# Attention step of a two-stage MoE kernel: weighted sums moved ahead of the query transpositions, PSUM pairs in rotation

## The chip, the core and the metric

The kernel runs on one core of a Trainium2 chip. The metric is the device time of one execution in microseconds (us). Five engines work beside each other, each in the order of its own instruction list: TensorE (PE in the profile: matrix products and transpositions, its weight loads are PEld), VectorE (DVE), ScalarE (ACT), GpSimd (POOL) and SyncE (SP), which here issues the DMA transfers. They wait for each other through semaphores. PE writes its results to PSUM, eight banks of 2 KB per partition; DVE and ACT read them from there. About 0.2% is what a measurement of this kernel can tell from no change.

## What is computed

The program is an attention with feature maps and, behind it, two mixtures of experts (MoE). The change touches the attention alone, which takes the first 145 us of some 1890. Its reference, for 4 batches, 8 heads, 576 tokens, head size 64 and 128 features:

```python
def phi(x):
    proj = np.einsum('bhsd,df->bhsf', x, w_phi)
    proj = proj - np.max(np.abs(proj), axis=-1, keepdims=True)
    return np.concatenate([np.exp(proj), np.exp(-proj)], axis=-1)
q_p, k_p = (phi(q), phi(k))
kv = np.einsum('bhsf,bhsd->bhfd', k_p, v)
z = np.sum(k_p, axis=2)
num = np.einsum('bhsf,bhfd->bhsd', q_p, kv)
den = np.einsum('bhsf,bhf->bhs', q_p, z)[..., None] + 1e-06
return (num / den).astype(np.float32)
```

Its result, as 2304 rows of 512, goes through a first MoE (all 8 experts on all rows, weighted by a balanced gate) and a second one (each row to its one best expert). These fill the rest of the time.

## The kernel before

The attention is cut into 8 units (two batches and two heads each), and a unit into 3 groups of 384 tokens. One step of the loop at L668 takes one group through every stage of a software pipeline (`step`, L624): the projection of a key group and of a query group (`proj`, L140), and for groups of earlier steps the key-value product (`kvm`, L163), the transposition of the query's projection (`qtr`, L183), the weighted sums (`num`, L195) and the transposition of the finished rows (`xtr`, L211). There are 24 key groups; query groups run two steps behind, so that a unit's key-value product is complete before its queries need it. Steps 4 to 24 of the loop have a `num` in this loop's main part, steps 5 to 24 also an `xtr`; from step 25 on (`live["tail"]`) the stages are interleaved with the first MoE's matmuls and use other PSUM tiles. In the names of tiles k and q stand for key and query; the first number after rk or rq is the unit, the second the group.

What a step makes each engine do:

- PE: k projection (12 records in the profile), q projection (12), key-value products (48 records, or 64 where the middle group of a unit crosses the border of two batches), 6 transpositions of `qtr`, 3 of `xtr`, 48 records of `num`.
- DVE: row maximum and subtraction for the key (`mk`, `prk`, L153 and L154) and the query (`mq`, `prq`), then for `num` the denominator, its reciprocal and the product (`d` and `xn`, L206 to L208). In steps 4 to 9 a few small operations of `misc_comp` come on top.
- ACT: exponentials of the key (`ek`, L158) and the query (`eq`, L192), once per unit two copies of the key-value product (`kvz`, L180), the copy of the transposed rows (`xo`, L218), and from step 12 casts of weights and rows for the MoE (L332, L369).

Before, the order within a step on PE is k, q, `kvm`, `qtr`, `xtr`, `num`. PSUM is used so: two pairs of banks (tag psR, two buffers) take k, q and `qtr` in turn; two single banks (psD) take `xtr` and `num` in turn; one bank each (psC, psB) holds the key-value sums of the unit. A PSUM tile can be given out again only when the readers of its last contents are done; the program puts such waits, and those for inputs, into the instruction that needs them. A tile is what the waits are made for: between two uses of one and the same tile by different engines the program orders the later behind the earlier.

`misc_trans` (L299) transposes an 8-row table of the second MoE once; the loop calls it ahead of step 6.

Of the kernel before, what the change touches and what calls it, by code (L numbers as in the profile page):

```python
# [11 lines left out]
F32 = mybir.dt.float32  # L12
# [9 lines left out]
B, H, S, D = 4, 8, 576, 64  # L22
NT = B * S
DM = H * D
E, FF = 8, 1024
P = 128
NTL = NT // P
KD = DM // P
# [16 lines left out]
def build(tc, a, out):  # L45
# [5 lines left out]
    live = {}  # L51
# [10 lines left out]
    n_ps = [0]  # L62

    def psum(tag, shape):
        n_ps[0] += 1
        bufs = {"A": 4, "B": 1, "C": 1, "D": 2}[tag]
        return live["pp"].tile(shape, F32, tag="ps" + tag, bufs=bufs, name=f"ps{tag}{n_ps[0]}")
# [31 lines left out]
    NG, NC = len(CH), len(CH[0])  # L99
    GW = NC * P  # L100
    S2 = 2 * S
    W = D + 1
# [12 lines left out]
        cs = slice(c0_ * W, c1_ * W)  # L115
        SP.dma_start(out=live["v", u][:, :, cs], in_=a["v"][bp, h_][:, :, cs])

    def heads2(tags):
        if not live.get("tail"):
            n_ps[0] += 1  # L120
            t = live["pp"].tile([P, 2, 512], F32, tag="psR", bufs=2, name=f"psR{n_ps[0]}")[:, :, 0:GW]
            return [t[:, 0], t[:, 1]], [(slice(0, 2), t)]
        ts = [psum(t_, [P, 1, GW]) for t_ in tags]
        return [t[:, 0] for t in ts], [(slice(h_, h_ + 1), t) for h_, t in enumerate(ts)]

    def warm(n):
        ps = psum("D", [P, P])
        for _ in range(n):
            T.matmul(ps, ident, ident, start=True, stop=True)

    wphi = ap_.tile([P, P], F32, bufs=1, name="wphi")
    load_in(0, "k", 0)
    for g in range(2):
# [2 lines left out]
    load_in(0, "k", 1)  # L136
    load_v(0, NC, 10)
    warm(8)

    def proj(u, which, g):  # L140
        r = live.pop(("r" + which, u, g))
        hs, parts = heads2("CB")
        for c in range(NC):
            for h_ in range(2):
                rs = slice(h_ * D, h_ * D + D)
                T.matmul(hs[h_][:, c * P:(c + 1) * P], r[rs, c * P:(c + 1) * P], wphi[rs, :], start=True, stop=True)  # L146
        m = ap_.tile([P, 2, NC], F32, tag="m", bufs=4, name=f"m{which}{u}{g}")
        pr = ap_.tile([P, 2, NC, P], F32, tag="pr" + which, name=f"pr{which}{u}{g}")
        if which == "k" and (u, g) == (0, 0):
            parts = [(slice(h_, h_ + 1), parts[0][1][:, h_:h_ + 1]) for h_ in range(2)]  # L150
        for h_, ps in parts:
            ps = ps.rearrange("p h (c f) -> p h c f", f=P)
            V.tensor_reduce(out=m[:, h_], in_=ps, axis=AX.X, op=ALU.max, apply_absolute_value=True)  # L153
            V.tensor_tensor(out=pr[:, h_], in0=ps, in1=m[:, h_].unsqueeze(3).to_broadcast([P, h_.stop - h_.start, NC, P]), op=ALU.subtract)  # L154
        if which == "k":
            ek = ap_.tile([P, 2, 2, NC, P], F32, tag="ek", name=f"ek{u}{g}")
            for h_, sg in [(h_, sg) for h_, _ in (parts if (u, g) == (0, 0) else [(slice(0, 2), None)]) for sg in range(2)]:
                A.activation(out=ek[:, sg, h_], in_=pr[:, h_], func=AF.Exp, scale=1.0 - 2.0 * sg)  # L158
            live["ek", u, g] = ek
        else:  # L160
            live["pr", u, g] = pr
# [15 lines left out]
    def kvcopy(u):  # L177
        kvz = ap_.tile([P, 2, 2, 2 * W], F32, tag="kvz", name=f"kvz{u}")
        for h_, ps in enumerate(live.pop(("kv", u))):
            A.copy(kvz[:, h_], ps)  # L180
        live["kvz", u] = kvz

    def qtr(u, g):  # L183
        pr = live.pop(("pr", u, g))
        eq = ap_.tile([P, 2, 2, GW], F32, tag="eq", name=f"eq{u}{g}")
        hs, parts = heads2("DD")
        for h_ in range(2):
            for c in range(NC):
                T.transpose(hs[h_][:, c * P:(c + 1) * P], pr[:, h_, c, :], ident)
        for sg in range(2):  # L190
            for h_, ps in parts:
                A.activation(out=eq[:, sg, h_], in_=ps, func=AF.Exp, scale=1.0 - 2.0 * sg)  # L192
        live["eq", u, g] = eq

    def num(u, g):  # L195
        eq, kvz = live.pop(("eq", u, g)), live["kvz", u]
        ps = psum("C" if live.get("tail") else "D", [P, 2 * NC, W])
        for ci, c in enumerate(CH[g]):
            for h_ in range(2):
                for sg in range(2):  # L200
                    for i, cs in enumerate(HALVES):
                        o = W * (2 * c + i > 8)
                        T.matmul(ps[cs, 2 * ci + h_, :], eq[:, sg, h_, ci * P + cs.start:ci * P + cs.stop], kvz[:, h_, sg, o:o + W], start=(sg == 0), stop=(sg == 1))  # L203
        d = ap_.tile([P, 2 * NC], F32, tag="d", name=f"d{u}{g}")
        xn = ap_.tile([P, 2 * NC, D], F32, tag="xn", name=f"xn{u}{g}")
        V.tensor_scalar_add(d, ps[:, :, D], 1e-6)  # L206
        V.reciprocal(d, d)
        V.tensor_tensor(out=xn, in0=ps[:, :, 0:D], in1=d.unsqueeze(2).to_broadcast([P, 2 * NC, D]), op=ALU.mult)  # L208
        live["xn", u, g] = xn

    def xtr(u, g):  # L211
        bp, h_ = units[u]
        xn = live.pop(("xn", u, g))
        ps = psum("B" if live.get("tail") else "D", [P, GW])
        for c in range(NC):
            T.transpose(ps[:, c * P:(c + 1) * P], xn[:, 2 * c:2 * c + 2, :].rearrange("p h e -> p (h e)"), ident)
        xo = ap_.tile([P, GW], F32, tag="xo", name=f"xo{u}{g}")
        A.copy(xo, ps)  # L218
        o = bp * S2 + g * GW
        SP.dma_start(out=xd[:, h_, o:o + GW], in_=xo)  # L220
# [76 lines left out]
        V.tensor_tensor(out=wgs[:, KD:2 * KD, E:2 * E], in0=wgx, in1=f32(wgs[:, KD:2 * KD, 0:E]), op=ALU.subtract)  # L297

    def misc_trans():  # L299
        ps = psum("D", [P, KD, E])  # L300
        for k in range(KD):
            T.transpose(ps[:, k, :], emb[:, k * P:(k + 1) * P], ident[0:E, 0:E])
        V.tensor_copy(enT, ps)
# [320 lines left out]
    def step(k, q, fill=None):  # L624
        def more(n=1):
            for _ in range(n if fill else 0):
                filled[0] += 1
                next(fill)

        ko, qo, no, xo_ = (pipe[c] for c in "kqnx")  # L630
        pipe.update(k=k, q=q, n=qo, x=no)
        if k:
            proj(k[0], "k", k[1])
        if q:
            proj(q[0], "q", q[1])
        more()
        if ko == (0, 0):
            warm(4)
        if ko:
            kvm(*ko)  # L640
        if qo:
            qtr(*qo)
        if ko and ko[1] == NG - 1:
            kvcopy(ko[0])
        more()
        if xo_:
            xtr(*xo_)
        if live.get("misc"):
            next(misc, None)
        if no:  # L650
            num(*no)
        more()

    misc = misc_comp()
# [4 lines left out]
    def at_(i):  # L659
        return order[i] if 0 <= i < len(order) else None  # L660
# [6 lines left out]
    i = 0  # L667
    while i < NU * NG + LAG or any(pipe.values()):  # L668
        p, g = divmod(i, NG)
        for which, nx in (("k", at_(i + 2)), ("q", at_(i + 2 - LAG))):  # L670
            if nx:
                load_in(nx[0], which, nx[1])
        if g == (1 if p else 2) and p + 1 < NU:
            load_v(p + 1)
        if i == NG:
            misc_loads()
        live["misc"] = i > NG
        if i == NG + 3:
            misc_trans()
        if i == 9:  # L680
            load_w(1, 0)
        if i == 12:
            live["o1"] = wops(1, 0)
            live["wsp"] = ap_
            bg.extend(partial(both, nm) for nm in ("A11 S1r", "S3r A12", "S2r S1 A22", "S4r S3", "S2 S4"))
            bg.append(partial(load_w, 2, 0))
        if i == 18:
            q = []
            for t_ in ("hB11", "hB21"):
                s_ = hp.tile([P, 2, 2, TH], F32, tag=t_, name="xs" + t_)  # L690
                q += [s_[:, 0], s_[:, 1]]
            ops = x_tasks(HS[0][1], q)
            ops["load"]()
            bg.extend(ops[k_] for k_ in XFIRST)
        if i == NU * NG + 1:
            while bg:
                bgpop()
            live["tail"] = True
            psum_pool("pp")
            psum("A", [P, TH])  # L700
            o2 = wops(2, 0, SL1)
            bg.extend(o2[nm] for nm in ("A11", "A12", "A21", "A22"))
        step(at_(i), at_(i - LAG), first if i > NU * NG else None)
        bgpop(2 if i >= 18 else 1)
        i += 1
# [609 lines left out]
    for h, (n, bi) in enumerate(HS):  # L1315
        nxt = HS[h + 1][1] if h + 1 < NH else bi
        if nxt != bi:
# [3 lines left out]
            else:  # L1321
                q = scratch(h)
# [56 lines left out]
    tail = route_steps(0, (1, 2, 4, 6, 8, 10), (1, 2, 3, 4, 5, 6), b=8, o=9, p=11, c=11, d=13, s=20, w=21, i=(22, 23, 24, 25, 26, 27))  # L1379
# [253 lines left out]
```

## Time and profile before

| | |
|---|---|
| median of 3 runs | 1892.92 us (1891.45 to 1895.74) |
| the profiled execution | 1889.36 us, of which span 1887.5 us |
| PE busy | 1870.1 us (99% of the span) |
| DVE / ACT / POOL busy | 1282.6 / 861.2 / 966.9 us |
| chain that ended last | PE 90%, issue 3%, DVE 3% |
| PE in 50 to 75 us (attention) | 24.95 of 25 us busy, clock 1.00 |
| first MoE matmul on PE | at 145.43 us |

The page counts an engine as busy while one of its instructions runs; PE's matmuls overlap, so that the start of one row to the start of the next tells more than the lengths. All rows below are of the profiled execution, in us from the start of its span.

### The profile page before, as it was taken

Reading aid. Unit: us, or ns where it says so; the run is one execution under the profiler, and the core shown is the slowest. Engines: PE = TensorE matmul, PEld = TensorE weight load, DVE = VectorE, ACT = ScalarE, POOL = GpSimd, SP = SyncE. Lnnn points to the kernel's source line nnn. Section 1 sums busy time; section 2 is a strip of 40 time slices with the busy share of each in tenths; the row PEclk is TensorE's granted clock in tenths of the full one; section 3 lists DMA queues with packets and bytes.
Section 4 is the critical chain, followed back from the end, with each engine's and each line's share of the span. In section 5 each row is a group of like instructions: output and inputs, shape, how many; then the busy total and the mean of one; then the engine's idle time right before and its main releaser. Section 6 shows DMA issues by size and latency. Waiting matters only on the chain.

```text
span 1887.5 us, 34736 instructions
## 1 busy us (share of the span) xinstructions
PE 1870.1 (99%) x13649; PEld 1795.7 (95%) x13649; DVE 1282.6 (68%) x1667; ACT 861.2 (46%) x1258; POOL 966.9 (51%) x687
## 2 busy tenths in 40 slices
PE   9999999999999999999999999999999999999998
PEld 8999999999999999999999999999999998788886
DVE  7775676766756657567566675665665647899995
ACT  5674342333333333424243333334242335889885
POOL 0241377846556564747474665657484733522220
PEclk9999999999999999999999999999999999999999
DMA  5474545536372736354463637273635353263950
GB/s 169 147 278 183 228 140 166 179 126 208 107 246 90 254 87 226 115 190 160 145 180 124 216 106 246 88 252 94 215 116 188 130 171 123 69 228 101 340 206 28
DMA packets 125161, 314.47 MB, mean 167 GB/s; under 512 B 23336, under 2 KB 72248, under 8 KB 124994
## 3 DMA queue, kind: packets, MB, share of 16 engines
q1 hardware_dynamic: 120898, 301.69, 47.2%
q0 software_dynamic: 4096, 10.51, 1.6%
q8 instruction: 110, 1.80, 0.4%
q14 instruction: 57, 0.47, 0.1%
HBM read 335.29 MB, written 32.44 MB: 195 GB/s over the span
## 4 chain that ended last, share of the span: by engine, by line
PE 90%; issue 3%; DVE 3%; DMA 1%; POOL 1%; ACT 1%; SPq 0%; POOLq 0%; DVEq 0%; ACTq 0%
PE Q L413 22%; PE Q L415 22%; PE Q L414 22%; PE psR L146 2%; PE psD L203 2%; PE psA L413 1%; PE psA L1214 1%; PE psA L1215 1%; PE psD L1248 1%; PE psD L1247 1%; PE psD L413 1%; PE psD L1246 1%; PE psA L1213 1%; PE psA L415 1%; PE psA L414 1%
## 5 line engine op out<-in xcount | busy, mean ns | idle before, releaser
L477 DVE TENSOR_TENSOR acca<-acca,Q 128x768 f32<-128x768 f32 x196 | 181.6, 949 | 131.0 <-PE Q L415 131.0
L461 POOL TENSOR_TENSOR hB<-rb,hB 128x768 fp32r<-128x768 f32 x42 | 77.6, 1848 | 181.9 <-ACT hB L458 181.9
L415 PE MATMUL Q<-xT,w1S 128*128 128x384 f32 x504 | 168.3, 334 | 0.0
L414 PE MATMUL Q<-hT,w2S 128*128 128x384 f32 x504 | 168.3, 334 | 0.0
L414 PE MATMUL Q<-xT,w1S 128*128 128x384 f32 x504 | 168.3, 334 | 0.0
L413 PE MATMUL Q<-hT,w2S 128*128 128x384 f32 x504 | 168.3, 334 | 0.0
L415 PE MATMUL Q<-hT,w2S 128*128 128x384 f32 x504 | 168.3, 334 | 0.0
L413 PE MATMUL Q<-xT,w1S 128*128 128x384 f32 x504 | 168.3, 334 | 0.0
L477 DVE TENSOR_TENSOR accb<-accb,Q 128x768 f32<-128x768 f32 x98 | 90.8, 948 | 66.4 <-PE Q L415 66.4
L473 DVE TENSOR_TENSOR Q<-Q,ra 128x768 f32<-128x768 f32 x42 | 40.6, 966 | 132.3 <-PE Q L415 130.9
L333 POOL TENSOR_TENSOR w1A<-raw,w1A 128x512 fp32r<-128x512 f32 x48 | 62.8, 1308 | 131.0 <-ACT w1A L332 131.0
L482 ACT COPY ra<-Q 128x768 f32<-128x768 f32 x42 | 33.6, 800 | 186.2 <-PE Q L415 184.7
L461 POOL TENSOR_TENSOR hT<-ra,hT 128x768 fp32r<-128x768 f32 x42 | 77.7, 1849 | 69.3 <-ACT hT L458 69.3
L415 PE MATMUL Q<-hB,w2A 128*128 128x384 f32 x338 | 113.0, 334 | 0.0
L413 PE MATMUL Q<-hB,w2A 128*128 128x384 f32 x338 | 112.9, 334 | 0.0
L414 PE MATMUL Q<-hB,w2A 128*128 128x384 f32 x338 | 112.9, 334 | 0.0
L414 PE MATMUL Q<-xB,w1A 128*128 128x384 f32 x336 | 112.2, 334 | 0.0
L415 PE MATMUL Q<-xB,w1A 128*128 128x384 f32 x336 | 112.2, 334 | 0.0
L413 PE MATMUL Q<-xB,w1A 128*128 128x384 f32 x336 | 112.2, 334 | 0.0
L1187 DVE TENSOR_TENSOR s1l<-rw,s1h 128x1024 fp32r<-128x1024 f32 x88 | 102.6, 1219 | 4.7 <-ACT s1h L1186 2.9
L473 DVE TENSOR_TENSOR Q<-Q,rc 128x768 f32<-128x768 f32 x42 | 40.6, 967 | 91.6 <-PE Q L415 91.6
L461 POOL TENSOR_TENSOR hT<-rd,hT 128x768 fp32r<-128x768 f32 x42 | 77.8, 1852 | 48.2 <-ACT hT L458 48.2
(477 smaller groups left out, 6118.9 us busy)
## 6 DMA issues: line engine op xcount, KB each, us to landing
xT<-xpd SPq DMA_DIRECT2D x120, 768.0 KB
rw<-in_moe_w SPq DMA_DIRECT2D x176, 512.0 KB
xB<-xpd SPq DMA_DIRECT2D x90, 768.0 KB
raw<-in_moe_w SPq DMA_DIRECT2D x34, 512.0 KB
gate<-gd SPq DMA_DIRECT2D x45, 384.0 KB
rx<-in_moe_w SPq DMA_DIRECT2D x30, 512.0 KB
xpd<-xT SPq DMA_DIRECT2D x12, 768.0 KB
xpd<-xB SPq DMA_DIRECT2D x9, 768.0 KB
```

The source lines that it names most:

```text
L146: T.matmul(hs[h_][:, c * P:(c + 1) * P], r[rs, c * P:(c + 1) * P], wphi[rs, :], start=True, stop=True)
L203: T.matmul(ps[cs, 2 * ci + h_, :], eq[:, sg, h_, ci * P + cs.start:ci * P + cs.stop], kvz[:, h_, sg, o:o + W], start=(sg == 0), stop=(sg = ...
L333: eng.tensor_tensor(out=t[:, 1], in0=r(nm), in1=f32(t[:, 0]), op=ALU.subtract)
L413: T.matmul(bank, w[:, 0, j, k, :], x[:, 0, k, :], start=start and k == 0, stop=False, skip_group_check=True)
L414: T.matmul(bank, w[:, 0, j, k, :], x[:, 1, k, :], start=False, stop=False, skip_group_check=True)
L415: T.matmul(bank, w[:, 1, j, k, :], x[:, 0, k, :], start=False, stop=stop and k == 1, skip_group_check=True)
L461: eng.tensor_tensor(out=hb[nm][:, 1], in0=src, in1=f32(hb[nm][:, 0]), op=ALU.subtract)
L473: V.tensor_tensor(out=out, in0=x, in1=y, op=op)
L477: V.tensor_tensor(out=z, in0=z, in1=ps, op=op)
L482: A.copy(m1c, b0)
L1187: V.tensor_tensor(out=lo, in0=r, in1=f32(hi), op=ALU.subtract)
L1213: T.matmul(ps[hf], th[:, k, :], wh[:, cs], start=(k == 0), stop=False)
```

## The change

`step` calls `num` right behind `kvm` and the copies `kvcopy`, then `xtr`, and `qtr` last. In place of two psR pairs and two psD banks there are three pairs (tags psR0 to psR2), which step i uses by turns: k takes pair i mod 3 and, later in the step, `qtr` takes the same pair; q takes pair i+1; `num` and `xtr` share one tile of pair i+2 (`sums`), `num` in its first bank and `xtr` in its second. `misc_trans` moves from the head of step 6 to behind that step's `xtr`, into the same tile. The few lines ahead of the loop fix which banks the pairs get. The tail keeps its order.

```diff
+    def pair3(k):
+        n_ps[0] += 1
+        return live["pp"].tile([P, 2, 512], F32, tag=f"psR{k % 3}", name=f"psR{n_ps[0]}")
+
-    def heads2(tags):
+    def heads2(tags, k=0):
         if not live.get("tail"):
-            n_ps[0] += 1
-            t = live["pp"].tile([P, 2, 512], F32, tag="psR", bufs=2, name=f"psR{n_ps[0]}")[:, :, 0:GW]
+            t = pair3(live["i"] + k)[:, :, 0:GW]
             return [t[:, 0], t[:, 1]], [(slice(0, 2), t)]
...
+    def sums():
+        if ("z", live["i"]) not in live:
+            live["z", live["i"]] = pair3(live["i"] + 2)
+        return live["z", live["i"]]
...
-        ps = psum("C" if live.get("tail") else "D", [P, 2 * NC, W])
+        ps = psum("C", [P, 2 * NC, W]) if live.get("tail") else sums()[:, 0, 0:2 * NC * W].rearrange("p (c w) -> p c w", w=W)
...
-        ps = psum("B" if live.get("tail") else "D", [P, GW])
+        ps = psum("B", [P, GW]) if live.get("tail") else sums()[:, 1, 0:GW]
...
-        if qo:
-            qtr(*qo)
         if ko and ko[1] == NG - 1:
             kvcopy(ko[0])
+        if not live.get("tail") and no:
+            num(*no)
+        if live.get("tail") and qo:
+            qtr(*qo)
         more()
         if xo_:
             xtr(*xo_)
+        if live["i"] == NG + 3:
+            misc_trans()
         if live.get("misc"):
             next(misc, None)
-        if no:
+        if live.get("tail") and no:
             num(*no)
+        if not live.get("tail") and qo:
+            qtr(*qo)
         more()
```

In the changed kernel the lines stand 13 to 17 lower: L159 is `proj`, L188 `kvm`, L202 `qtr`, L216 `num`, L229 `xtr`, L315 `misc_trans`.

PE's list in step 10, from the key group of unit 3, group 1 (rk31) to the next (rk32), behind the last products of `kvm`; brackets name the engines or DMA queues whose semaphore an instruction waits for. Before:

```order
L175 MATMUL psB49_1038<-v3_681,ek30_915 64x65 x2
L189 MATMUL psR50_1064<-ident_68,prq21_926 128x128 [waits DVE_49,PE_49]
L189 MATMUL psR50_1064<-ident_68,prq21_926 128x128 x5
L216 MATMUL psD51_1073<-ident_68,xn12_1002 128x128 [waits Activation_49]
L216 MATMUL psD51_1073<-ident_68,xn12_1002 128x128 x2
L203 MATMUL psD52_1080<-kvz2_963,eq20_953 64x65 x24
L146 MATMUL psR53_1114<-wphi_93,rk32_896 128x128 [waits DMAHW7_49,DVE_49,PE_49]
```

and now:

```order
L188 MATMUL psB48_1037<-v3_683,ek30_915 64x65 x2
L216 MATMUL psR49_1062<-kvz2_953,eq20_995 64x65 [waits PE_49,Activation_49]
L216 MATMUL psR49_1062<-kvz2_953,eq20_995 64x65 x23
L229 MATMUL psR49_1062<-ident_68,xn12_982 128x128 [waits DVE_49]
L229 MATMUL psR49_1062<-ident_68,xn12_982 128x128 x2
L202 MATMUL psR50_1099<-ident_68,prq21_926 128x128 [waits PE_49]
L202 MATMUL psR50_1099<-ident_68,prq21_926 128x128 x5
L159 MATMUL psR51_1112<-wphi_98,rk32_896 128x128 [waits DMAHW7_49,PE_49]
```

`num` stands ahead of both transpositions, `xtr` writes the tile of `num` (psR49 in both) and has a wait for DVE, and `qtr` and the next k projection have lost theirs.

PE's list at the start, step 3 (rk10 and rq01 are its projections). Before:

```order
L146 MATMUL psR9_291<-wphi_93,rk10_167 128x128 [waits DMAHW0_49,DVE_49,PE_49]
L146 MATMUL psR9_291<-wphi_93,rk10_167 128x128 x5
L146 MATMUL psR10_305<-wphi_93,rq01_169 128x128 [waits DMAHW1_49,DVE_49,PE_49]
L146 MATMUL psR10_305<-wphi_93,rq01_169 128x128 x5
L175 MATMUL psC5_190<-v0_98,ek02_233 64x65 [waits Activation_49]
```

and now:

```order
L159 MATMUL psR14_296<-wphi_98,rk10_172 128x128 [waits DMAHW0_49,DVE_49,PE_49]
L159 MATMUL psR14_296<-wphi_98,rk10_172 128x128 x5
L159 MATMUL psR15_310<-wphi_98,rq01_174 128x128 [waits DMAHW1_49]
L159 MATMUL psR15_310<-wphi_98,rq01_174 128x128 x5
L188 MATMUL psC10_195<-v0_103,ek02_238 64x65 [waits Activation_49]
```

The k projection of step 3 now takes the pair that the q projection of step 2 (rq00) wrote, where before it took that of step 2's k projection; the q projection has no wait for DVE any more.

PE's list in step 6, behind its `num`, with the transposed table (embt). Before, `misc_trans` stood at the step's head:

```order
L203 MATMUL psD22_535<-kvz0_350,eq01_410 64x65 x24
L302 MATMUL psD23_569<-ident_68,embt_143 128x8 [waits DVE_49,Activation_49]
L302 MATMUL psD23_569<-ident_68,embt_143 128x8 x3
L146 MATMUL psR24_575<-wphi_93,rk20_353 128x128 [waits DMAHW7_49]
L146 MATMUL psR24_575<-wphi_93,rk20_353 128x128 x5
```

and now it stands behind `xtr`:

```order
L229 MATMUL psR29_625<-ident_68,xn01_546 128x128 [waits DVE_49]
L229 MATMUL psR29_625<-ident_68,xn01_546 128x128 x2
L315 MATMUL psR29_625<-ident_68,embt_148 128x8 [waits Activation_49]
L315 MATMUL psR29_625<-ident_68,embt_148 128x8 x3
L202 MATMUL psR30_670<-ident_68,prq10_485 128x128 [waits PE_49]
```

It writes the same tile (psR29) as `num` and `xtr` and waits for ACT.

## Rows read from the trace of the kernel before

**Rows 1.** The page: busy time, share of the span and instructions of each engine.

```profile
PE 1870.1 (99%) x13649; PEld 1795.7 (95%) x13649; DVE 1282.6 (68%) x1667; ACT 861.2 (46%) x1258; POOL 966.9 (51%) x687
```

**Rows 2.** Busy time by stretch: length; PE, PEld, DVE, ACT, POOL (instructions); clock, DMA share, GB/s.

```profile
50.00:75.00 25.00, 24.95 (x556) 23.12 (x556) 19.82 (x35) 14.81 (x26) 0.00 (x0) 1.00 0.52 167
```

**Rows 3.** Timeline of PE, step 9: start, length, line, tiles, records.

```profile
49.87 0.94 PE L146 MATMUL psR<-wphi,rk 64*128 64x128 f32 x12
...
51.41 0.34 PE L175 MATMUL psC<-v,ek 128*64 128x65 f32 x4
...
52.74 0.29 PE L175 MATMUL psB<-v,ek 128*64 128x65 f32 x4
53.04 0.85 PE L189 MATMUL psR<-ident,prq 128*128 128x128 f32 x6
53.72 0.49 PE L216 MATMUL psD<-ident,xn 128*128 128x128 f32 x3
54.15 1.62 PE L203 MATMUL psD<-kvz,eq 128*64 128x65 f32 x48
55.69 0.94 PE L146 MATMUL psR<-wphi,rk 64*128 64x128 f32 x12
```

**Rows 4.** Timeline of PE, step 8, a long one.

```profile
43.63 0.94 PE L146 MATMUL psR<-wphi,rk 64*128 64x128 f32 x12
...
46.97 0.29 PE L175 MATMUL psB<-v,ek 128*64 128x65 f32 x4
```

**Rows 5.** Timeline of DVE, step 9.

```profile
50.88 0.95 DVE L153 TENSOR_REDUCE mk<-psR 128x6 f32<-128x768 f32 x1
...
53.79 0.96 DVE L154 TENSOR_TENSOR prq<-psR,mq 128x768 f32<-128x768 f32 x1
54.67 0.18 DVE L295 TENSOR_TENSOR wgs<-wgt,wgs 128x32 fp32r<-128x32 f32 x1
...
55.81 0.17 DVE L206 TENSOR_SCALAR d<-psD 128x6 f32<-128x6 f32 x1 [0.65 <-PE psD L203]
...
56.24 0.56 DVE L208 TENSOR_TENSOR xn<-psD,d 128x384 f32<-128x384 f32 x1
```

**Rows 6.** Waits of PE over the whole span: us in total, times, longest us.

```profile
PE psA L1195 <- DMA xgs<-x2d,idt: 3.9, 1, 3.9
PE psB L1150 <- DVE ohs L1145: 0.7, 1, 0.7
```

**Rows 7.** Timeline of the start, PE (steps 3, 4, 5), then DVE.

```profile
15.47 0.94 PE L146 MATMUL psR<-wphi,rq 64*128 64x128 f32 x12 [0.26 <-PE psR L146]
...
19.25 0.94 PE L146 MATMUL psR<-wphi,rk 64*128 64x128 f32 x12 [0.49 <-PE psR L189]
...
25.19 0.94 PE L146 MATMUL psR<-wphi,rk 64*128 64x128 f32 x12
...
14.41 0.96 DVE L154 TENSOR_TENSOR prq<-psR,mq 128x768 f32<-128x768 f32 x1
...
20.23 0.96 DVE L153 TENSOR_REDUCE mk<-psR 128x6 f32<-128x768 f32 x1 [1.08 <-PE psR L146]
...
24.03 0.67 DVE L274 TENSOR_TENSOR embt<-embt 8x512 f32<-8x512 f32 x1
```

**Rows 8.** Timeline of PE ahead of step 6, and of ACT in step 13.

```profile
31.66 0.41 PE L302 MATMUL psD<-ident,embt 8*128 8x8 f32 x4 [0.16 <-ACT xo L218]
32.00 0.94 PE L146 MATMUL psR<-wphi,rk 64*128 64x128 f32 x12
...
78.13 1.49 ACT L192 ACTIVATE eq<-psR 128x768 f32<-128x768 f32 x2
79.51 0.48 ACT L218 COPY xo<-psD 128x384 f32<-128x384 f32 x1
```

**Rows 9.** Busy time by stretch around the longest wait of PE, columns as in rows 2.

```profile
1600.00:1610.00 10.00, 6.61 (x92) 5.12 (x90) 7.46 (x7) 8.12 (x12) 4.03 (x6) 1.00 0.29 81
1610.00:1620.00 10.00, 9.51 (x76) 8.24 (x76) 5.86 (x13) 6.01 (x11) 4.92 (x9) 0.83 0.16 31
```

More of the change, by code (lines that the diff above doesn't have):

```diff
@@ L124, in heads2 @@
         return [t[:, 0] for t in ts], [(slice(h_, h_ + 1), t) for h_, t in enumerate(ts)]
+    def sums():
+        if ("z", live["i"]) not in live:
+            live["z", live["i"]] = pair3(live["i"] + 2)
+        return live["z", live["i"]]
     def warm(n):
-        ps = psum("D", [P, P])
+        ps = pair3(2)[:, 0, 0:P]
         for _ in range(n):
             T.matmul(ps, ident, ident, start=True, stop=True)
+    for k in (1, 2):
+        pair3(k)
+    for t_ in "CB":
+        psum(t_, [P, 1])
+    pair3(0)
     wphi = ap_.tile([P, P], F32, bufs=1, name="wphi")
@@ L141, in proj @@
         r = live.pop(("r" + which, u, g))
-        hs, parts = heads2("CB")
+        hs, parts = heads2("CB", which == "q")
         for c in range(NC):
@@ L299, in misc_trans @@
     def misc_trans():
-        ps = psum("D", [P, KD, E])
+        ps = sums()[:, 1, GW:GW + KD * E].rearrange("p (k e) -> p k e", e=E)
         for k in range(KD):
@@ L676, in build @@
             misc_loads()
-        live["misc"] = i > NG
-        if i == NG + 3:
-            misc_trans()
+        live["misc"], live["i"] = i > NG, i
         if i == 9:
```

## The prediction, made before the changed kernel ran

> **What bounds the kernel now.** I read the busy times first: PE is busy 1870 us of 1887 [rows 1]; in the attention it is 24.95 of 25 us at the full clock [rows 2]. The timeline of PE then gives one step of the loop piece by piece, from start to start [rows 3]: a k projection begins at 49.87 and the next at 55.69, 5.82 us later, and in between every piece starts where the last leaves off. A step whose key-value product has 64 records instead of 48 takes 49.87 - 43.63 = 6.24 us [rows 3, 4]. The timeline of DVE says how close behind it follows [rows 5]: mk starts 1.01 us into the step and the chain mk, prk, mq, prq lets go of DVE 3.79 us later (50.88 to 54.67); d, reciprocal and xn take 0.99 us (55.81 to 56.24 + 0.56). DVE has slack before, because nobody on PE needs xn until the next step.
>
> So PE's order and PE's waits alone set the end of the attention, and what follows is PE too: its largest wait after it is 3.9 us [rows 6]. A microsecond lost here is lost at the end.
>
> **What the change adds: a wait inside every step.** In the built program the first transposition of xtr waits for DVE, and the count it waits for is the one that the xn of the same step raises: num and xtr now share one tile of two banks, DVE reads num's half, and xtr writes the tile after that in program order. The list of PE shows it indirectly too: the next k projection, whose pair was last read by prq, no longer waits for DVE, since the wait at xtr already covers it. Before, xtr had a bank of its own and needed only the xn of the step before. Behind the waiting xtr stand qtr and the whole next step on PE, and behind the next k projection stands DVE's next chain. PE and DVE, which ran beside each other, now take turns.
>
> A short step. The last key-value pair begins at 52.74, with room for two such pairs until 52.86 (the records of this group come 0.12 apart by fours), so num now begins 2.99 into the step [rows 3]. Before, d came 1.66 after num's start (54.15 to 55.81) [rows 3, 5]; without the pause of some 0.05 with which num entered after a transposition, 1.61. That would let d start at 4.60. DVE: mk follows the k projection by 0.98 (19.25 to 20.23) [rows 7], and 0.98 + 3.79 = 4.77, so DVE decides. xn ends at 5.76. PE starts 0.10 after a DVE end it waits for (14.41 + 0.96 = 15.37, to 15.47) [rows 7]: xtr at 5.86. The nine transpositions and the pause behind them take 54.15 - 53.04 = 1.11 [rows 3]: next k projection at 6.97, where it was 5.82. That is +1.15.
>
> A long step. num begins at 46.97 + 0.12 - 43.63 = 3.46 [rows 4], d at 5.07 (now PE decides), xn ends at 6.06, xtr at 6.16, next step at 7.27 against 6.24: +1.03. Step 24 has no k projection, so there too PE decides when d starts: +1.0 by the same sum.
>
> Steps 7 to 23 are 11 short and 6 long ones: 11 x 1.15 + 6 x 1.03 = 18.8 us.
>
> **The start.** In step 3 the k projection takes the pair of step 2's q projection and waits for prq, which ends at 15.37; it starts at 15.47, where before it was the q projection that waited for the same end [rows 7]. DVE's mk comes 0.98 later, at 16.45, prq starts 2.91 behind it [rows 5] and ends at 20.32, and step 4's k projection starts at 20.42 instead of 19.25. Step 4 has no xtr, so it takes 5.82 less xtr's 0.43 (53.72 to 54.15), 5.4: step 5 starts at 25.8 instead of 25.19 [rows 3, 7]: +0.6. In step 5, misc_comp's two operations of 0.67 hold DVE 1.3 us behind xn; mk starts at 27.4 instead of 26.8, d at 31.2, xtr at 32.3, step 6 at 33.4 instead of 32.00 [rows 8]: +0.8 more. In step 6 misc_trans stands behind xtr and waits for ACT's copy xo, since it writes the tile that xo reads: xtr at 5.86 runs 0.49 [rows 3], the copy 0.48 [rows 8], 0.10 to PE, misc_trans 0.34 (31.66 to 32.00) [rows 8], then qtr and the pause, 0.8: 8.0 against 5.82, +2.2.
>
> **Saved.** Putting num behind kvm drops one change between kinds of matmul per step: the pauses at them are 53.04 - 52.86 = 0.18, and about 0.1 in front of num and of the projection. Some 0.15 us a step; it is already in the sums above, where num begins at 2.99. The first projections that waited for eq no longer do; that is in the start.
>
> **Costed at nothing.** ACT's xo now waits for xn and stands ahead of eq: xtr ends at 6.35, xo at 6.8, and the next q projection, which waits for it, starts at 6.97 + 0.77 = 7.74 (0.77 is half of 51.41 - 49.87 [rows 3]). eq takes 1.49 [rows 8] and ends near 8.4, num needs it at 6.97 + 2.99 = 9.96. The cover is 0.9 and 1.5 us; gone, the step grows by what is missing. The tail's order is unchanged, and its first tiles are read long before. SP's transfers keep their order.
>
> **Sum.** 0.6 + 0.8 + 2.2 + 18.8 + 1.0 = 23.4 us, on 1889.36 us of the profiled execution: 1912.8. That execution lies 3.6 us under the median of the runs shown (1892.92), and a measurement will be a median: 1892.9 + 23.4 = 1916.3, say 1916. The unknowns are small ones: 0.05 us a step in DVE's pitch and in the semaphores is 1 us in all; the start may be 1.5 us off; a part of PE's later waits (3.9 and less) may shrink by as much as it starts late, or not. Own range 1910 to 1922.
>
> **Rivals.**
>
> Rival 1, the wait does not bind, and the saving alone is left. For it: the banks differ, and DVE has slack. Against it: the wait is in the program. Then a step saves the dropped change, 0.15 to 0.18; 20 steps give some 3.3 us, and the start comes out even, since step 3's later projection is made up for by the waits for eq and xo that go [rows 7, 8]: 1889.6, a gain of 0.17%, at the edge of what can be told. The decisive point is whether xtr starts before xn has ended. By the Trainium skill (PSUM — Partial Sum Buffer, section on PSUM bank collisions) access has to be guarded by bank and quadrant, and other engines may use different banks at once: by that rule alone xtr in its own bank needs no wait and the result is this rival's. The rows cannot show it, as before the two had different tiles; I give it 0.05.
>
> Rival 2, the clock falls. PE now pauses 1.3 us in each 7. After the 3.9 us wait near 1610 the granted clock was 0.83 over the next 10 us, a mix of its two levels, 1.2 and 2.4 GHz; a wait of 0.7 us left no such mark [rows 6, 9]. At 1.2 GHz a short step's PE part before d doubles, 4.6 to 9.2, xn ends at 10.2, the transpositions take 2.2: 12.5 a step, +6.7, over 20 steps +134: 2027. The pause lies nearer to 0.7 than to 3.9, and PE works four fifths of the time; 0.04. The Trainium skill (TensorE: Matmul & The Clock Gate, section on HAM oscillation) warns that idle gaps between bursts of matmuls throw the clock back; no row here shows it for gaps of this length.
>
> Rival 3, ACT becomes the bound in the steps with casts for the MoE. Without casts ACT works 14.81 of 25 us [rows 2], 3.4 of a short step; the casts of steps 12 to 23 come on top, and xo and eq now stand in one forced order behind xn. If xo comes late by more than the cover of 0.9 us, say by 0.5 more in 12 steps, PE loses 6 us on top: 1922, and with 1.0 more 1928. Against it: a step of 6.97 us is more room than the 5.82 that held the same work. 0.08.
>
> **How the numbers follow.** Forecast 0.83, rival 1 0.05, rival 2 0.04, rival 3 0.08. The range of 8 in 10 is the forecast's with half of rival 3: 1909 to 1926. Slower by over 0.2% (3.8 us; less than that a measurement of this kernel cannot tell from no change) holds in all but rival 1: 0.95; rival 1 splits into 0.02 faster and 0.03 the same.
>
> **What would show it.** In the changed profile PE's waits have a row of xtr (L229) behind DVE's xn (L221), some 20 times 1.2 to 1.4 us; a short step is 6.97 us long, a long one 7.27, the third step of three no longer stands out; DVE's d follows prq without a gap in short steps; the first MoE matmul on PE moves from 145.4 to about 168.8, and behind it the distances stay as they were. A start of xtr before xn's end refutes the forecast; a clock under 1.00 between 30 and 165 us speaks for rival 2; xo ending after 7.6 us into a step for rival 3.

## The result, and the profile after

The changed kernel takes 1917.39 us (median of 6 runs, 1915.61 to 1919.01); the kernel before, run beside it, 1894.11 us (median of 6). The ratio is 1.0124, 95% interval 1.0112 to 1.0136: slower by 23.3 us, where 23.4 was forecast and 1916 us in all. The execution profiled took 1916.59 us, its span 1914.8.

The page's first part: PE's busy time is what it was [rows 1], in a span that is 27 us longer.

```profile
PE 1870.7 (98%) x13649; PEld 1796.1 (94%) x13649; DVE 1284.6 (67%) x1667; ACT 865.4 (45%) x1258; POOL 967.0 (51%) x687
```

Busy time by stretch, same columns as in [rows 2]: PE, which had no gap in the attention, now has 4.7 us of them in 25, at an undiminished clock.

```profile
50.00:75.00 25.00, 20.33 (x486) 18.91 (x483) 17.31 (x33) 12.72 (x19) 0.00 (x0) 1.00 0.46 145
```

The waits of PE over the whole span (us in total, times, longest) name the gaps.

```profile
PE psR L229 <- DVE xn L221: 22.5, 19, 1.3
...
PE psR L229 <- DVE wgt L291: 1.5, 1, 1.5
...
PE psR L315 <- ACT xo L231: 0.6, 1, 0.6
```

L229 is `xtr`: 20 of its starts wait for DVE, for the `xn` of the same step. In step 5 the view names `wgt` (L291), which DVE ran next; but `misc_comp` stands behind `xtr` in the program, and there too `xtr` (31.16) follows the end of `xn` (30.55 + 0.56 = 31.11) by 0.05. The timeline of PE, the end of step 8 and step 9, answers to [rows 3, 4]:

```profile
47.23 0.94 PE L159 MATMUL psR<-wphi,rk 64*128 64x128 f32 x12
...
54.47 0.94 PE L159 MATMUL psR<-wphi,rk 64*128 64x128 f32 x12
...
57.46 1.57 PE L216 MATMUL psR<-kvz,eq 128*64 128x65 f32 x48
60.28 0.55 PE L229 MATMUL psR<-ident,xn 128*128 128x128 f32 x3 [1.25 <-DVE xn L221]
...
61.41 0.38 PE L159 MATMUL psR<-wphi,rk 64*128 64x128 f32 x2
```

A short step is 61.41 - 54.47 = 6.94 us (6.97 forecast, 5.82 before), a long one 54.47 - 47.23 = 7.24 (7.27 and 6.24). `num` begins 57.46 - 54.47 = 2.99 into the short one, as in the prediction's sum. DVE in step 9, which answers to [rows 5]:

```profile
58.38 0.96 DVE L167 TENSOR_TENSOR prq<-psR,mq 128x768 f32<-128x768 f32 x1
59.25 0.15 DVE L219 TENSOR_SCALAR d<-psR 128x6 f32<-128x6 f32 x1
...
59.67 0.56 DVE L221 TENSOR_TENSOR xn<-psR,d 128x384 f32<-128x384 f32 x1
```

`d` follows `prq` without a gap, so in a short step it is DVE's chain that sets when `xn` ends (60.23), behind which PE starts `xtr` at 60.28: the two engines take turns. In the start, the k projections of steps 5 to 7 answer to [rows 7, 8]:

```profile
24.68 0.94 PE L159 MATMUL psR<-wphi,rk 64*128 64x128 f32 x12
...
32.30 0.94 PE L159 MATMUL psR<-wphi,rk 64*128 64x128 f32 x12
...
40.37 0.94 PE L159 MATMUL psR<-wphi,rk 64*128 64x128 f32 x12
```

and in the kernel before, step 7 began here:

```profile
37.80 0.38 PE L146 MATMUL psR<-wphi,rk 64*128 64x128 f32 x2
```

Step 5 is 7.62 us long and step 6 8.07, where before they took 6.81 and 5.80. From the first key-value product to the first piece of the tail the attention takes 22.6 us more than before: 0.5 up to step 5, 0.8 in step 5, 2.3 in step 6, 18.1 in steps 7 to 23, 1.0 in step 24.

In absolute time the first MoE matmul moved by less, from 145.43 to 167.08 us (168.8 forecast), because the first key-value product began 1.0 us earlier in this execution (7.75 us, before 8.72). The distance between the two executions then stays at 21.7 to 22.0 us up to 1550 us; 5.4 us more are lost behind that, where the kernels are the same. In the changed kernel's profile the clock stands lower there in some stretches, as in this one:

```profile
1630.00:1640.00 10.00, 5.55 (x88) 4.64 (x87) 5.34 (x6) 5.73 (x9) 3.83 (x7) 0.79 0.31 83
```

The profile before lost the clock once [rows 9]. All nine kernels below lose time there as the changed one does, by 2.4 to 7.3 us against the profile before, which is shorter than every timed run of its kernel (1891.45 and more). So I put this part down to the execution; of the difference of the medians, 23.3, the attention has the 22.6.

### The profile page after: what moved, and what is told of

The parts are those of the page before. It is cut to its first block, busy times and chain, and to the rows that moved or that the text cites. A ratio compares the mean times of both kernels' runs of the same rounds, so it can differ in the third digit from the quotient of the medians.

```text
span 1914.8 us, 34751 instructions
## 1 busy us (share of the span) xinstructions
PE 1870.7 (98%) x13649; PEld 1796.1 (94%) x13649; DVE 1284.6 (67%) x1667; ACT 865.4 (45%) x1258; POOL 967.0 (51%) x687
## 4 chain that ended last, share of the span: by engine, by line
PE 89%; DVE 5%; issue 3%; DMA 1%; POOL 0%; ACT 0%; SPq 0%; POOLq 0%; DVEq 0%; ACTq 0%
PE Q L426 21%; PE Q L427 21%; PE Q L428 21%; PE psD L1265 2%; PE psA L1232 2%; PE psA L1231 2%; PE psD L1264 2%; PE psA L1230 2%; PE psD L1263 2%; PE psD L426 1%; PE psR L159 1%; PE psA L426 1%; PE psD L428 1%; PE psD L427 1%; PE psA L428 1%
```

## The experiments

Nine kernels were run. Each is the changed kernel with one edit, where not said otherwise; what decides in the rows is the start of one k projection to the next.

### 1. DVE reads `num` after `xtr` in program order

```diff
-            num(*no)
+            rd = num(*no)        # the matmuls alone
...
-            xtr(*xo_)
+            xrd = xtr(*xo_)      # the transpositions alone
+        if not live.get("tail") and no:
+            rd()                 # d, reciprocal, xn
+        if xo_:
+            xrd()                # xo
```

> The changed kernel, with one thing else: DVE's three reads of num's half (d, reciprocal, xn) are placed behind xtr's transpositions in program order, and ACT's copy xo behind these. PE's order and the banks stay. Theory A (the 23 us are xtr's wait for the xn of its own step, which is there only because xtr writes the tile that DVE has just read): xtr then has nothing to wait for, the 19 waits of about 1.2 us in front of it go. What is left is the next q projection's wait for xo: num ends 4.6 us into a short step, xtr 5.0, xn 6.1, xo 6.7, and the q projection could start at 6.4, so 0.3 us a step: 5.97 us instead of 6.94, some 0.15 above before's 5.82; with the start, 1894 to 1899 us. Rival B (the new order of pieces itself, or the later eq and xo, cost the time): PE's order is unchanged, so 1913 to 1919. Rival C (a lower clock after pauses): also near 1917 only if the pauses stay; with them gone as A, so the granted clock in the attention decides (1.00 in the changed kernel).

Measured: 1901.89 us, ratio 1.0045 (1.0030 to 1.0061). PE's waits in the attention, and its timeline in one short step:

```profile
PE psR L159 <- ACT xo L238: 4.3, 16, 1.1
```

```profile
78.73 0.94 PE L159 MATMUL psR<-wphi,rk 64*128 64x128 f32 x12
79.86 0.94 PE L159 MATMUL psR<-wphi,rq 64*128 64x128 f32 x12 [0.19 <-ACT xo L238]
82.18 1.57 PE L216 MATMUL psR<-kvz,eq 128*64 128x65 f32 x48
83.68 0.55 PE L232 MATMUL psR<-ident,xn 128*128 128x128 f32 x3
...
84.81 0.94 PE L159 MATMUL psR<-wphi,rk 64*128 64x128 f32 x12
```

`xtr` (L232 here) follows `num` at once: no row of a wait for `xn` is left, though order, banks and arithmetic are the changed kernel's. So what `xtr` waited for was not data: it transposes the `xn` of the step before. It was the rule that a later write of a tile stands behind its earlier readers. The time missed its range by 3 us. The step is 6.08 where 5.97 was expected, since the q projection waits for `xo` as foreseen and somewhat longer (`xo` starts after `xn`, and then 0.48 us). Step 6 takes 8.21 us (5.80 before), with a wait of 1.64 us of `misc_trans` for `xo`; and behind it, in step 7, the clock fell (0.93 over 25 to 50 us), and that step takes 7.18. Theory A holds, B falls. C was the clock: it had no part in the changed kernel's attention (1.00).

### 2. `qtr` ahead of `xtr`

```diff
-        if live.get("tail") and qo:
+        if qo:
             qtr(*qo)
...
-        if not live.get("tail") and qo:
-            qtr(*qo)
```

> The changed kernel with qtr ahead of xtr in every step (key-value products, num, qtr, xtr). The wait for the same step's xn stays, but 0.8 us of PE's own work now stands in it. Theory A: xtr starts at 5.86 us into a short step as before, the next k projection 0.5 behind it, at 6.35 (changed kernel 6.94, before 5.82); a long step 6.65 (7.24 and 6.24). Over 20 steps 12 us less than the changed kernel: 1903 to 1908 us. Rival B (order or ACT): xtr's copy xo comes a little later and eq earlier; no gain of this size, 1912 to 1919.

Measured: 1915.00 us, ratio 1.0112 (1.0097 to 1.0128), a miss. The wait for `xn` did shrink; the timelines of PE and of ACT show another in its place:

```profile
59.20 0.55 PE L229 MATMUL psR<-ident,xn 128*128 128x128 f32 x3 [0.28 <-DVE xn L221]
59.68 0.94 PE L159 MATMUL psR<-wphi,rk 64*128 64x128 f32 x12
60.96 0.94 PE L159 MATMUL psR<-wphi,rq 64*128 64x128 f32 x12 [0.34 <-ACT xo L231]
...
66.41 0.94 PE L159 MATMUL psR<-wphi,rk 64*128 64x128 f32 x12
```

```profile
59.02 1.51 ACT L205 ACTIVATE eq<-psR 128x768 f32<-128x768 f32 x2 [0.91 <-PE psR L202]
60.42 0.48 ACT L231 COPY xo<-psR 128x384 f32<-128x384 f32 x1
```

With `qtr` its exponentials moved ahead too, so `xo` stands behind 1.5 us of `eq` in ACT's list, and the next q projection wants the pair that `xo` reads: it starts 1.28 us behind the k projection instead of 0.77. 6.73 us a step instead of 6.35. Theory A had moved PE's instructions and not ACT's. Rival B, whose range (1912 to 1919) holds, had named `xo` and `eq`, but gave no sum for them.

### 3. The same with `xo` ahead of `eq` on ACT

The edit, against experiment 2; `qtr` now returns the exponentials as a function (cut here):

```diff
-            qtr(*qo)
+            ex = qtr(*qo)
+            if live.get("tail"):
+                ex()
...
             xtr(*xo_)
+        if qo and not live.get("tail"):
+            ex()
```

> The run with qtr ahead of xtr missed its forecast: it waited 0.28 us for xn (19 times, as 0.45 was expected) and 0.38 us for xo (17 times) in front of the q projection, as eq (1.5 us) now stood ahead of xo in ACT's order. Here qtr stays ahead of xtr, but ACT runs xo first and eq behind it. Theory A with ACT's order: xo then ends 0.6 us behind xtr and before the q projection wants its pair; the step goes from 6.73 to 6.35 us (long 7.19 to 6.75), 1906 to 1910 us. Rival: the wait for xo is not due to ACT's order but to xo's wait for xn: stays near 1915.

Measured: 1903.95 us, ratio 1.0057 (1.0040 to 1.0074), 2 us better than the range. PE in a short step:

```profile
78.12 0.94 PE L159 MATMUL psR<-wphi,rk 64*128 64x128 f32 x12
78.90 0.85 PE L159 MATMUL psR<-wphi,rq 64*128 64x128 f32 x12
...
83.93 0.55 PE L232 MATMUL psR<-ident,xn 128*128 128x128 f32 x3 [0.43 <-DVE xn L224]
84.41 0.71 PE L159 MATMUL psR<-wphi,rk 64*128 64x128 f32 x8
```

The q projection waits for nothing and the step is 6.29 us: the order of `xo` and `eq` on ACT is worth some 11 us. What is left of the wait for `xn`, 0.43, is the 1.25 of the changed kernel less the 0.8 that `qtr` covers: a wait of known place and size can be filled with work that is due anyway.

### 4. One tile for each bank

```diff
-        return live["pp"].tile([P, 2, 512], F32, tag=f"psR{k % 3}", name=f"psR{n_ps[0]}")
+        return [live["pp"].tile([P, 1, 512], F32, tag=f"psR{k % 3}{h_}", name=f"psR{n_ps[0]}_{h_}") for h_ in range(2)]
...
```

The other lines of the edit, cut here, take one of the two tiles where they took a half of the pair.

> The changed kernel's order and rotation, but each pair of banks is two tiles of one bank, so that num and xtr have a tile each and nothing false is waited for. DVE's and ACT's operations that took both heads in one now take one head each (four short ones more on DVE and two on ACT per step). Theory A: PE waits for neither xn nor xo in a step; PE's own work sets 5.67 us a short step (5.82 less one change between kinds of matmul, 0.15), and the attention ends some 3 us before that of the kernel before: 1889 to 1893 us. DVE's added operations are hidden as long as its chain stays under 5.6 us a step (4.78 now plus some 0.25). Rival B (the order costs): 1905 or more. Rival D (the split operations make DVE or ACT the bound): 1900 to 1915, with PE waiting for DVE in front of the projections.

Measured: 1899.13 us, ratio 1.0022 (1.0012 to 1.0032). PE in a short step, and two of PE's waits:

```profile
57.83 0.94 PE L159 MATMUL psR<-wphi,rk 64*128 64x128 f32 x12
...
60.87 1.57 PE L216 MATMUL psR<-kvz,eq 128*64 128x65 f32 x48
62.38 0.55 PE L229 MATMUL psR<-ident,xn 128*128 128x128 f32 x3
...
63.51 0.49 PE L159 MATMUL psR<-wphi,rk 64*128 64x128 f32 x4
```

```profile
PE psR L315 <- ACT xo L231: 1.1, 1, 1.1
PE psR L159 <- DMA rq<-in_qT: 0.9, 1, 0.9
```

With the banks tracked apart the new order runs at 5.68 us a step (5.62 in other short ones, 6.09 in the ordinary long ones), 0.15 to 0.21 less than before. That is the size the prediction gave to the change between kinds of matmul that the new order drops (three a step are left of four). By the Trainium skill (TensorEngine Tiling (Array Packing), section Tiling Modes) a change of tiling mode drains TensorE; the shorter steps agree, though no run isolates one change. The gain, some 3 us over the steps, is lost again in single places: `misc_trans` behind `xo` in step 6, a late load, pauses that the profile calls issue, and the start; from the first key-value product to the tail the attention takes 2.8 us more than before. Another 2.4 us are lost between 170 and 300 us, in the first MoE, where one such pause takes 1.4 us; the changed kernel has none there. So B falls a second time, and A's time is missed by 6 us. Rival D's range (1900 to 1915) begins just above the result, but its sign is almost missing: PE waits for DVE in front of a projection twice, 1.3 us in all, both in the start.

### 5. The same, with `misc_trans` between `num` and `d`

```diff
-        ps = sums()[1][:, 0, GW:GW + KD * E]...
+        ps = sums()[0][:, 0, 2 * NC * W:2 * NC * W + KD * E]...
...
+        en = misc_trans() if live["i"] == NG + 3 else None
         d = ap_.tile([P, 2 * NC], F32, tag="d", name=f"d{u}{g}")
...
+        if en:
+            en()                 # the copy enT, behind xn
```

> The run with tiles of one bank had ordinary steps of 5.62 to 5.68 and 6.09 us (before: 5.83 and 6.24), which is 3 us gained in the attention, but gave it back in single steps: 7.69 us in the sixth, where misc_trans waited 1.1 us for xo and DVE for misc_comp, and pauses and late loads of 0.7 to 0.9 in three others. Here misc_trans writes the free end of num's bank, between num and d, so that it waits for nothing, and the copy of its result stands behind xn. Theory A: the sixth step falls to about 6.1 us, so 1.5 us less than that run's 1899: 1896 to 1899, still not below the kernel before, since the late loads and pauses come with the faster steps and stay. Rival: those pauses were chance and differ from run to run: then 1891 to 1895, at or just below the kernel before.

Measured: 1895.43 us, ratio 1.0008 (0.9999 to 1.0017): not to be told from the kernel before. The k projections of steps 6 and 7:

```profile
32.78 1.14 PE L159 MATMUL psR<-wphi,rk 64*128 64x128 f32 x12
39.15 0.94 PE L159 MATMUL psR<-wphi,rk 64*128 64x128 f32 x12
```

That is just under theory A's range (1896 to 1899) and just over the rival's (1891 to 1895). Step 6 is 6.37 us, 1.3 less than in experiment 4 (6.1 was expected). Two long steps, 14 and 20, are again longer than 6.09: 6.82 and 7.25 us here, 7.10 and 6.76 in experiment 4. As they are the same two, the pauses are hardly chance in place, though their sizes differ; what PE's issue waits for there stays open. The late load of experiment 4 did not come again. No run beat the kernel before.

### 6. Only the banks, in the old order

```diff
-        if not live.get("tail") and no:
-            num(*no)
-        if live.get("tail") and qo:
+        if qo:
             qtr(*qo)
...
-        if live.get("tail") and no:
+        if no:
             num(*no)
```

> Only the half of the change that concerns the banks: three pairs in turn and num and xtr in one tile, but PE's pieces in the order of before (key-value products, qtr, xtr, num). Theory A in its wide form (what costs is the shared tile, whichever order): now num, which writes the tile after xtr, waits for ACT's copy xo of it, 0.1 + 0.48 + 0.1 = 0.65 us a step, and the next q projection, which takes the pair, waits for xn, 0.35 us: about 1 us a step, 1908 to 1919 us. Rival B (the order of the pieces costs, not the tile): 1891 to 1896, as before.

Measured: 1956.73 us, ratio 1.0326 (1.0310 to 1.0342). The direction is A's, the size is not. PE's waits over the span, then ACT and PE in one step:

```profile
PE psR L216 <- ACT xo L231: 35.9, 19, 2.2
```

```profile
57.94 1.51 ACT L205 ACTIVATE eq<-psR 128x768 f32<-128x768 f32 x2 [0.43 <-PE psR L202]
59.34 0.49 ACT L231 COPY xo<-psR 128x384 f32<-128x384 f32 x1
```

```profile
59.88 1.62 PE L216 MATMUL psR<-kvz,eq 128*64 128x65 f32 x48 [1.71 <-ACT xo L231]
```

`num` now writes the tile that `xo` reads, and `xo` again stands behind `eq`: 1.9 us a step instead of 0.65. The same omission as in experiment 2. The waits for `xo` are 36 of the 63 us. The q projection waits another 4.6 us, `misc_trans` 2.2, and with these pauses the clock also fell, again and again (0.86 over 75 to 100 us); how the rest divides is not told apart here.

### 7. Only the order, with the old banks (the kernel before, edited)

```diff
-        if qo:
-            qtr(*qo)
         if ko and ko[1] == NG - 1:
             kvcopy(ko[0])
+        if not live.get("tail") and no:
+            num(*no)
...
+        if not live.get("tail") and qo:
+            qtr(*qo)
```

> The kernel before, with only the order of PE's pieces changed (key-value products, num, xtr, qtr); pools as before, so num and xtr have a bank each, and the projections and qtr take two pairs in turn. Theory A (the 23 us need both: num ahead of xtr, and one tile for them): PE does not wait for xn. But the pair of the next q projection is now the one that qtr has just filled: num, xtr and qtr take 5.67 us of a step, eq ends at 7.25 to 7.35, and the q projection could start at 6.44, so it waits 0.9 us in every step, a wait of another kind: 6.57 us a short step, 1908 to 1914 us, with the waits in front of the q projection behind eq and none in front of xtr. Rival B (the order costs by itself, through more than waits): PE's pauses would be in front of num or xtr.

Measured: 1908.79 us, ratio 1.0081 (1.0064 to 1.0098). PE's largest wait:

```profile
PE psR L146 <- ACT eq L192: 15.0, 19, 0.8
```

As expected: nothing in front of `xtr`, 0.79 us for `eq` in front of 19 q projections. Both halves alone are slower than before (by 15.7 and 63 us). I read that so: the three pairs are the remedy for this wait of the new order, and the one tile for `num` and `xtr` comes with the third pair; experiment 4 shows that its two banks need not be one tile.

### 8. DVE's `xn` twice, in the changed kernel and in the kernel before

```diff
         V.tensor_tensor(out=xn, in0=ps[:, :, 0:D], in1=d.unsqueeze(2).to_broadcast([P, 2 * NC, D]), op=ALU.mult)
+        V.tensor_tensor(out=xn, in0=ps[:, :, 0:D], in1=d.unsqueeze(2).to_broadcast([P, 2 * NC, D]), op=ALU.mult)
```

In the changed kernel:

> The changed kernel with DVE's xn written twice in every step, the same operation again (0.56 us each in the trace of the changed kernel). Theory A: xtr waits for the second, so each of the 21 steps in which it waits grows by 0.56 us or somewhat more (0.56 to 0.62): 11.8 to 13 us over the changed kernel, 1928 to 1932. Rival B or C (order, clock): DVE's operation is hidden as it would be in the kernel before, 1915 to 1919.

Measured: 1935.03 us, ratio 1.0214 (1.0195 to 1.0234), 17.6 us over the changed kernel. PE in one step, and busy time over another:

```profile
94.16 0.94 PE L159 MATMUL psR<-wphi,rk 64*128 64x128 f32 x12
...
100.56 0.55 PE L230 MATMUL psR<-ident,xn 128*128 128x128 f32 x3 [1.84 <-DVE xn L222]
...
101.69 0.49 PE L159 MATMUL psR<-wphi,rk 64*128 64x128 f32 x4
```

```profile
70.00:79.00 9.00, 7.32 (x131) 6.79 (x133) 5.21 (x8) 3.64 (x7) 0.00 (x0) 0.81 0.46 146
```

The ordinary step goes from 6.94 to 7.53: +0.59 for an operation of 0.56, as A has it (20 steps wait, not 21). The result is 3 us above A's range, and the excess over the expected 12 us is in the main the clock: with waits of 1.7 to 2.2 us it fell in 6 of the 20 steps (0.81 in this stretch, 1.00 where the steps are ordinary). These are 1.4 to 2.1 us longer still; in the first of them, step 5, 0.6 of it is the added `xn` of step 4, which delays `mk`. What the prediction's rival 2 feared did not come with the change, and came in part with a wait half as long again.

In the kernel before:

> The kernel before with the same operation twice. There DVE's chain is 4.78 us of a step of 5.83, and nothing on PE needs xn before the next step: with 0.56 more it is 5.34 and stays hidden, 1892 to 1897 us. If DVE were already in PE's way before the change, it would take up to 0.56 us a step here too: 1904 and more.

Measured: 1900.53 us, ratio 1.0040 (1.0026 to 1.0054), a miss: between the two forecasts. DVE and PE in one step:

```profile
77.58 0.56 DVE L209 TENSOR_TENSOR xn<-psD,d 128x384 f32<-128x384 f32 x1
78.06 0.95 DVE L153 TENSOR_REDUCE mk<-psR 128x6 f32<-128x768 f32 x1
79.11 0.96 DVE L154 TENSOR_TENSOR prk<-psR,mk 128x768 f32<-128x768 f32 x1
```

```profile
76.45 0.94 PE L146 MATMUL psR<-wphi,rk 64*128 64x128 f32 x12
...
80.21 0.85 PE L189 MATMUL psR<-ident,prq 128*128 128x128 f32 x6 [0.61 <-DVE prk L154]
...
82.86 0.83 PE L146 MATMUL psR<-wphi,rk 64*128 64x128 f32 x10
```

DVE is busy for 5.11 us of this step and yet sets its length, 6.41 us (5.82 before, so the whole 0.56 and a little more shows): `num` ends the step on PE, `d`, `xn`, `mk` and `prk` follow on DVE, `qtr` takes the pair that `prk` reads, and `xtr` and `num` follow it. That is a ring through both engines. DVE's idle share says nothing about the slack in it.

## Why the prediction was right, and where not

The mechanism and its price were right. That the difference of the medians (23.3) agrees with the forecast (23.4) to 0.1 us is in part luck: the attention took 22.6 us more, 0.8 under the sum, and the rest lies within what medians differ by.

- **What bounds it, and the added wait**: right in place and cause. Experiment 1 takes the wait away by program order alone, 4 by tiles alone, and 8 lengthens it by what is added to DVE. The shared tile makes it, not the bank: `num` and `xtr` lie in different banks throughout. Rival 1's rule by banks holds only for a program that tracks banks, as experiment 4 does; even there, at 1899 and 1895, it did not give the 1889.6 of that rival.
- **The short and the long step**: 6.94 and 7.24 us, 0.03 under the sums, mostly because `xtr` starts 0.05 behind the end of `xn` (60.23 to 60.28) and not 0.10. DVE decides in the one, PE in the other, as worked out. Steps 7 to 23: 18.1 of 18.8 forecast.
- **The start**: 0.5, 0.8 and 2.3 us for 0.6, 0.8 and 2.2. Step 6 holds `misc_trans`' wait for `xo`, 0.6.
- **Saved**: `num` begins 2.99 into the step, as summed; 0.15 us a step was the low end of what experiment 4 showed, 0.15 to 0.21.
- **Costed at nothing**: right, with a slightly thinner cover than the text had. In step 10, as in the other ordinary short steps, `xo` ends 67.85 + 0.48 - 61.41 = 6.92 us into the step, not at 6.8, and the q projection comes at 7.7: 0.8 us of cover, not 0.9. Step 9 is the exception: there `xo` comes 0.3 later, for a reason that these rows do not show, and the cover is 0.5. ACT's timeline of the changed kernel, `xo` of steps 9 and 10:

```profile
61.20 0.48 ACT L231 COPY xo<-psR 128x384 f32<-128x384 f32 x1 [1.57 <-PE psR L229]
...
67.85 0.48 ACT L231 COPY xo<-psR 128x384 f32<-128x384 f32 x1 [1.81 <-PE psR L229]
```

  Experiments 2 and 6 show what the order of `xo` and `eq` is worth when it is reversed. Rival 3 did not come: no wait for `xo` or `eq` stands in front of a projection.
- **"DVE has slack before"**: wrong, though no term of the sum rested on it (rival 1 named it in its favour). The `xn` that step 9's `num` feeds ends 1.11 us into step 10, and `mk` can start some 1.01 into a step [rows 3, 5]: there is no slack at that place, as experiment 8 found at 0.4%.
- **Rival 2**: the clock stayed at 1.00 at waits of 1.25 us in 6.94 and did not at 1.84 in 7.53. By the Trainium skill (TensorE: Matmul & The Clock Gate, section on HAM oscillation) gaps between bursts throw the clock back; of the runs here that holds for the longer waits alone, those of 1.6 us and more in experiments 1, 6 and 8.

## What to carry to other kernels

When two stages share a tile, ask of every later writer which readers stand ahead of it in program order, even where banks and data have nothing to do with each other; the wait is removed by emitting the reads later or by separate tiles (here neither made the kernel faster than it had been), and its price is the ring through both engines, not the busy time of one. When an instruction is moved on one engine, move in the sum everything that it drags along on the others: here the order of two operations on ACT was worth some 11 us. A wait that cannot be removed can be filled with work that is due anyway, and after each such repair the next wait in the ring has to be looked up anew.

## What the runs showed of the hardware that was not expected

PE's clock tolerated 20 waits of 1.1 to 1.5 us in the attention (1.00 throughout) but fell in 6 of 20 steps when the waits were 1.7 to 2.2 us, and once behind a single wait of 1.64 us (experiment 1). The clock also fell behind 1550 us, where PE waits 3 to 6 us for a load, in every profile but in other stretches; what is lost there differs by up to 7.3 us between two executions. And the start of a run scatters: the first key-value product began at 8.72 us before and 7.75 after, and anywhere between in the other profiles.
